# A fused attention and gated-convolution kernel: a new order of TensorE's work, with fp32 runs joined, and a planner rule that marks more row copies as urgent

## The chip, the cores and the metric

One core of one Trainium2 chip runs the whole problem. The metric is the time of one execution on the device in microseconds (us). The kernel before takes 423.37 us, the median of three runs (422.53 to 424.21).

The engines by the names that the profile uses: PE is TensorE (PEld are its weight loads), DVE is VectorE, ACT is ScalarE, POOL is GpSimd, SP is SyncE, which here issues all the transfers but one. "q" behind a name (SPq) is the part of an engine that waits and issues.

## The reference

Agent attention over 4 batches of 12800 positions with 128 channels and 49 agents, followed by a gated convolution over positions:

```python
def _attn_ref(q, k, v, agents):
    a2k = sm(agents, k)                 # softmax over the 12800 keys
    agent_v = a2k @ v                   # 49 x 128
    q2a = sm(q, agents)                 # softmax over the 49 agents
    return q2a @ agent_v

def _moe_ref(x, w_val, conv_w, w_out):  # x is the attention's output
    for k in range(5):                  # causal convolution, 5 taps, per channel
        gate_pre += conv_w[k] * xp[:, k:k + S, :]
    gate = 1.0 / (1.0 + np.exp(-gate_pre))
    val = x @ w_val
    return (gate * val) @ w_out
```

## The kernel before

**Units and chunks.** Each batch is cut into 10 units of 1280 positions for keys, values and queries, and into 25 chunks of 512 positions for the gated convolution. The names in the order string of lines 1103 to 1129 are: `k1.8` the scores of key unit 8 of batch 1, `v` the agents' sums over a value unit, `q` the scores of a query unit and its softmax, `t` the transposition of that softmax, `m` a step of the key maximum, `f` a step that folds a batch's agent values into the convolution's weights, and `g`, `a`, `o` the gate, value and output products of a chunk, numbered 0 to 100 (the last chunk is cut in two).

**What is fp32 and what is 16-bit.** Scores (line 391) and value sums (line 495) multiply fp32 operands; so do the small products of `m` and most of `f`. The gate (lines 937, 941), value (964, 968) and output products (1007 to 1009) and the transposes multiply fp16 operands. A chunk is eleven 16-bit products, each with 512 columns. An fp32 run is a stretch of TensorE's order in which one fp32 product follows another, between two 16-bit ones.

**Banks.** All score units of keys and queries take turns on two PSUM banks (`bank()`, line 252; `sc` in the rows), so a score unit needs the bank of the unit two places ahead of it. A key unit's bank is given back by ScalarE's copy (line 417), a query unit's by VectorE's transpose (line 401). `gate`, `val` and `out` have one bank each: the gate of the next chunk needs the tanh of this one (line 950, ScalarE), its value product needs `h` (line 977, VectorE), and the output product needs `hh` (983, ScalarE) and `hl` (988, GpSimd).

**The path of a query unit.** Scores, transpose on VectorE, maximum, subtraction on GpSimd (765), exponential on ScalarE (773), sums and scaling on VectorE (778 to 787), a 16-bit copy on ScalarE (794) and two rests on GpSimd (800, 808) fill `pt`. From unit 4 of batch 0 on, a transfer transposes `pt` into the rows `x1` (849). Two units are a pair and serve five chunks. Of a pair, two further transfers, the row copies (`shifts`, line 880; issued at 898), set 19 of the rows at five shifts into `x2`, which line 941 multiplies. A pair's copies cover both of its units, but for units 0 to 3 of batch 0, which have copies of their own.

**What sets the order.** TensorE's order is the string. All other steps, the transfers among them, are ordered by `Plan.order` (line 97): it plays the steps through with written-in durations; of the steps that an engine could start now, it takes the one with the largest tail, which is the sum of costs along the longest way from the step to the end. The argument `urge` is added to a step's tail (line 114), and so to the tails of all that lead to it. `SOON` is 10. What comes out is a fixed order per engine, and each engine, and SP's transfer queue, keeps its order: a step that waits holds back all that stand behind it on its engine. At most eight of SP's transfers are on their way at a time; loads go round eleven buffers.

The lines that the change touches:

```python
                src, [("x2", s % 3, o + i * UNIT, r0) for i in range(n)], us * n,
                urge=SOON if g < SINGLE else 0.0,
            )
```

Of the kernel before, what the change touches and what calls it, by code (L numbers as in the profile page):

```python
# [49 lines left out]
SINGLE = 4  # L50
# [13 lines left out]
SOON = 10.0  # L64
# [6 lines left out]
class Plan:  # L71
# [11 lines left out]
    def add(self, engine, us, fn, reads=(), writes=(), moved=0.0, key=None, urge=0.0):  # L83
        i = len(self.steps)
        need = set()
        for x in reads:
            need |= self.wrote.get(x, set())
        for x in writes:
            need |= self.wrote.get(x, set()) | self.read.get(x, set())
        for x in reads:  # L90
            self.read.setdefault(x, set()).add(i)
        for x in writes:
            self.wrote[x], self.read[x] = {i}, set()
        self.steps.append((engine, us, fn, need, moved, key))
        self.urge.append(urge)
# [84 lines left out]
def tile_agent_attention_gated_conv(  # L180
# [10 lines left out]
    B, C, N = qT.shape  # L191
    A = 49
    NU = N // UNIT
# [19 lines left out]
    m2 = const.tile([P, 2], F32, name="m2")  # L213
# [610 lines left out]
    def row_keys(s, halves):  # L824


        i = s % NX
        return [(x, i, h) for h in halves for x in ("x1", "x1b")] + [("x1h", i)] * (0 in halves)

    def halo(s, read=()):  # L830
        to = x1s[s % NX][:, PAD - HALO : PAD]
        if s * 2 % NU == 0:
            fn = lambda: nc.gpsimd.memset(to, 0.0)
        else:
            fn = lambda: nc.gpsimd.tensor_copy(
                out=to, in_=x1s[(s - 1) % NX][:, PAD + SEG - HALO : PAD + SEG]
            )
        keys = [(x, (s - 1) % NX, 1) for x in ("x1", "x1b")]
        add("pool", 0.19, fn, list(read) + keys, [("x1h", s % NX)])

    def transposes(b, u):
# [3 lines left out]
        if not on_pe(b, u):  # L845
            dst = unit_rows(g)
            add(
                "dma", 1.4,
                lambda: nc.sync.dma_start_transpose(
                    out=dst.rearrange("p (n i) -> p n i", i=P),  # L850
                    in_=pt.rearrange("p n r -> p (n r)"),
                ),
                [(*p_, n) for n in range(3)], [("x1", g // 2 % NX, g % 2)], 2.4,
            )
            shifts(b, u)
            return
# [4 lines left out]
        def matmuls():  # L861
# [14 lines left out]
            [at], [("x1b", g // 2 % NX, g % 2)],  # L876
        )
        shifts(b, u)

    def shifts(b, u):  # L880

        g = b * NU + u
        if g >= SINGLE and g % 2 == 0:
            return
        n = 1 if g < SINGLE else 2
        u0 = u + 1 - n
        s = g // 2
        x2, x1 = x2s[s % 3], x1s[s % NX]
        o = (g + 1 - n) % 2 * UNIT
        src = row_keys(s, range(0, g % 2 + 1))  # L890
        c = PAD - HALO + o
        for r0, r1, first, every, us in X2CUTS:
            first += A
            rows = x1[first : first + 1 + (r1 - r0 - 1) * every : every, c : c + 1]
            view = [rows.ap[0], (1, TAPS), (1, n * UNIT)]
            add(
                "dma", 0.6,
                lambda r0=r0, r1=r1, rows=rows, view=view: nc.sync.dma_start(
                    out=x2[X2B + r0 * TAPS : X2B + r1 * TAPS, o : o + n * UNIT],
                    in_=bass.AP(rows.tensor, rows.offset, view),  # L900
                ),
                src, [("x2", s % 3, o + i * UNIT, r0) for i in range(n)], us * n,
                urge=SOON if g < SINGLE else 0.0,
            )
        if g % 2 and g < SINGLE:
            halo(g // 2 + 1)
# [165 lines left out]
    for b in range(B):  # L1072
        t0 = b * NCH
        for i in range(NU):
            g = b * NU + i + LEAD
# [17 lines left out]
    for t in range(len(chunks) + 2):  # L1093
# [9 lines left out]
    order = (  # L1103
# [25 lines left out]
    )  # L1129
    first = [(kinds.get(x[0], x[0]), *map(int, x[1:].split("."))) for x in order.split()]  # L1130
    for w in first:
# [70 lines left out]
```

## Time and profile before

| | |
|---|---|
| median of 3 runs | 423.37 us |
| the profiled execution, its own time | 419.86 us |
| span of its instructions | 417.9 us |
| mean granted TensorE clock | 0.996 |
| PE busy | 399.7 us, 96% |
| ACT busy | 307.2 us, 74% |
| DVE busy | 295.2 us, 71% |
| POOL busy | 237.4 us, 57% |

A row of the timeline gives the start of an instruction (or of a merged group of them, xN) from the span's start, its length, engine, line, operation and tiles; in square brackets stands how long the engine had been idle, and what ended that. Lengths of matmuls overlap, since they are pipelined: how fast TensorE goes is read from one start to the next. A row of waits names who waited, for whom, and how long in total. The page's groups give the busy time and the mean length of one, and then the idle time ahead of them with what ended most of it.

### The profile page before, as it was taken

To read this page: it belongs to the slowest core of one execution; us is meant where nothing else is said; L and a number is where in the kernel's file an instruction comes from. 1 tells how busy PE (TensorE), PEld (TensorE's weight loads), DVE (VectorE), ACT (ScalarE), POOL (GpSimd) and SP (SyncE) were. 2 spreads that over 40 slices of the span, in tenths; PEclk is the share of its full clock that TensorE was granted. 3 is DMA by queue.
4 is the path that set the end of the run, shared out by engine and by line. 5 is a ranking of instruction groups with operands and counts; after the bars stand their busy time and mean duration, and the time that the engine had idled before them with its cause. 6 is when DMAs were issued, how large, how long until landed. Compare 5 with 4: busy or idle time off the path is not lost.

```text
span 417.9 us, 10098 instructions
## 1 busy us (share of the span) xinstructions
PE 399.7 (96%) x3907; PEld 195.2 (47%) x3907; DVE 295.2 (71%) x570; ACT 307.2 (74%) x524; POOL 237.4 (57%) x303
## 2 busy tenths in 40 slices
PE   4978999999999999999999999999999999999995
PEld 1357334336555443345555543344555544344443
DVE  5866889976885977677796685777757598666231
ACT  6584468778957677678987486778877577788775
POOL 1002458655677566564476555585366577787643
PEclk9989999999999999999999999999999999999999
DMA  8999999999999999999999999999999977663823
GB/s 323 418 417 413 356 361 353 303 338 319 413 334 281 284 321 373 354 264 348 352 399 288 279 320 380 295 350 276 323 350 347 271 204 224 187 173 145 247 107 126
DMA packets 75131, 127.63 MB, mean 305 GB/s; under 512 B 50466, under 2 KB 50850, under 8 KB 75084
## 3 DMA queue, kind: packets, MB, share of 16 engines
q1 hardware_dynamic: 74940, 126.87, 96.3%
q8 instruction: 30, 0.49, 0.5%
q10 hardware_dynamic: 144, 0.13, 0.1%
q14 instruction: 17, 0.14, 0.1%
HBM read 79.25 MB, written 26.21 MB: 252 GB/s over the span
## 4 chain that ended last, share of the span: by engine, by line
PE 78%; DMA 11%; DVE 6%; ACT 1%; issue 1%; SPq 1%; POOL 0%; POOLq 0%; DVEq 0%
PE gate L937 24%; PE sc L391 17%; PE av L495 8%; DMA ld<-vP 6%; PE val L964 5%; PE out L1007 5%; PE gate L941 5%; PE val L968 5%; PE out L1008 5%; PE out L1009 4%; DMA ld<-kT 2%; DMA x<-pt 2%; DMA x<-x 1%; DVE h L977 1%; DVE sT L401 1%
## 5 line engine op out<-in xcount | busy, mean ns | idle before, releaser
L988 POOL TENSOR_TENSOR hl<-h,hh 128x512 f16<-128x512 f32 (+1 forms) x101 | 116.7, 1156 | 97.1 <-ACT hh L983 96.8
L937 PE MATMUL gate<-x,stat 128*128 128x512 f16 (+1 forms) x500 | 124.2, 378 | 0.4 <-ACT th L950 0.3
L977 DVE SCALAR_TENSOR_TENSOR h<-th,val 128x512 f32<-128x512 f32 x100 | 67.8, 678 | 62.1 <-PE out L1008 28.3
L391 PE MATMUL sc<-ld,ag_sb 128*32 128x320 f32 x1280 | 101.4, 447 | 7.3 <-DMA ld<-kT 6.7
L950 ACT ACTIVATE th<-gate,unscale 128x512 f32<-128x512 f32 x100 | 68.3, 683 | 32.7 <-PE gate L941 31.3
L1021 ACT ACTIVATE ob<-out,oscale 128x512 f32<-128x512 f32 x98 | 67.2, 686 | 19.1 <-PE out L1009 16.5
L937 PEld LDWEIGHTS <-stat 128*128 128x128 f16 x505 | 46.1, 97 | 63.3 <-issue 13.1
L983 ACT CAST hh<-h 128x512 f16<-128x512 f32 (+1 forms) x101 | 61.4, 608 | 16.6 <-DVE h L977 16.1
L765 POOL TENSOR_TENSOR qw<-sT,qmx 128x490 f32<-128x490 f32 x40 | 41.3, 1034 | 45.0 <-DVE qmx L760 44.7
L391 PEld LDWEIGHTS sc<-ld,ag_sb 128*32 128x32 f32 x1280 | 36.8, 111 | 58.7 <-issue 25.6
L495 PE MATMUL av<-ld,eT 128*32 128x129 f32 (+1 forms) x1400 | 49.6, 276 | 1.5 <-DVE eT L401 1.2
L495 PEld LDWEIGHTS av<-ld,eT 128*32 128x32 f32 (+1 forms) x1400 | 45.6, 115 | 8.4 <-issue 3.0
L808 POOL TENSOR_TENSOR pt<-qw,pt 128x490 f16<-128x490 f32 x40 | 44.8, 1119 | 1.6 <-ACT pt L794 1.4
L401 DVE STREAM_TRANSPOSE sT<-sc 128x640 f32<-128x640 f32 x40 | 33.5, 837 | 12.9 <-PE sc L391 12.2
L486 ACT ACTIVATE e<-ks,kbias 128x320 f32<-128x320 f32 x80 | 39.2, 553 | 3.5 <-DVE eT L401 2.2
L800 POOL TENSOR_SCALAR pt<-qw 128x240 f16<-128x240 f32 x80 | 27.8, 367 | 22.0 <-DVE qw L787 22.0
L401 DVE STREAM_TRANSPOSE eT<-e 128x640 f32<-128x640 f32 x40 | 33.3, 839 | 9.5 <-ACT e L486 5.3
L941 PE MATMUL gate<-x,stat 128*128 128x512 f16 x100 | 37.8, 378 | 0.5 <-DMA x<-x 0.5
L964 PE MATMUL val<-x,stat 128*128 128x512 f16 x100 | 37.9, 379 | 0.2 <-DVE wo L743 0.2
L968 PE MATMUL val<-x,stat 128*128 128x512 f16 x100 | 37.8, 378 | 0.0
L417 ACT COPY ks<-sc 128x640 f32<-128x640 f32 x40 | 27.6, 690 | 13.4 <-PE sc L391 13.0
L1007 PE MATMUL out<-hh,wo 128*128 128x512 f16 x98 | 37.2, 380 | 0.1
(133 smaller groups left out, 418.9 us busy)
## 6 DMA issues: line engine op xcount, KB each, us to landing
ld<-kT SPq DMA_DIRECT2D x40, 640.0 KB
ld<-qT SPq DMA_DIRECT2D x40, 640.0 KB
ld<-vP SPq DMA_DIRECT2D x39, 645.0 KB
outT<-ob SPq DMA_DIRECT2D x48, 512.0 KB
x<-x SPq DMA_DIRECT2D x18, 300.0 KB
x<-x SPq DMA_DIRECT2D x18, 175.0 KB
outT<-ob SPq DMA_DIRECT2D x3, 256.0 KB
ld<-vP SPq DMA_DIRECT2D x2, 322.5 KB
```

What stands on the lines that cost most here:

```text
L391: nc.tensor.matmul(out=out[g * BLK : (g + 1) * BLK, j, 0:GT], lhsT=ag_sb[:, b, j * BLK : (j + 1) * BLK], rhs=src[:, g * GT : (g + 1) * GT] ...
L401: nc.vector.transpose(out=out.rearrange("p n (j i) -> p j n i", j=2), in_=in_.rearrange("p j (n i) -> p j n i", i=BLK),)
L495: nc.tensor.matmul(out=av[o + j : o + j + cols, 0 : C + 1], lhsT=et[:, n, j : j + cols], rhs=vt[:, n, :], start=(u == 0 and n < 2), stop=( ...
L937: nc.tensor.matmul(out=pg, lhsT=stat[:, k, :], rhs=x1[:, c : c + w], start=(k == 0), stop=False,)
L941: nc.tensor.matmul(out=pg, lhsT=stat[:, TAPS + 1, :], rhs=x2[:, o2 : o2 + w], start=False, stop=True,)
L950: lambda: nc.scalar.activation(out=th, in_=pg, func=AF.Tanh, scale=unscale[:, 0:1]),
L964: nc.tensor.matmul(out=pv, lhsT=stat[:, TAPS, :], rhs=x1s[(b * NCH + n0 // CH) // 5 % NX][:, PAD + o2 : PAD + o2 + w], start=True, stop=False,
L968: nc.tensor.matmul(out=pv, lhsT=stat[:, TAPS + 2, :], rhs=x2[:, o2 : o2 + w], start=False, stop=True,)
L977: lambda: nc.vector.scalar_tensor_tensor(out=h, in0=th, scalar=1.0, in1=pv, op0=ALU.add, op1=ALU.mult),
L983: "act", 0.16 + 0.42 * scale, lambda: nc.scalar.copy(out=hh, in_=h),
L988: lambda: nc.gpsimd.tensor_tensor(out=hl, in0=h, in1=hh, op=ALU.subtract),
L1021: lambda: nc.scalar.activation(out=ob[:, o : o + w], in_=po, func=AF.Copy, scale=oscale),
```

## The change

Two things. The order string is written anew: every product is the same, but steps change places, so that fp32 products that stood apart stand side by side. And the row copies that carry `urge` are no longer those of units 0 to 3 alone, but those of units 4 and 5 too, and those of the last pair (units 8 and 9) of batches 0, 1 and 2.

```diff
-                urge=SOON if g < SINGLE else 0.0,
+                urge=SOON if g < SINGLE + 2 or u == NU - 1 and b < B - 1 else 0.0,
...
-        "q0.7 k1.6 o3 k1.7 g5 o4 a5 g6 k1.8 a6 t0.6 t0.7 k1.9 g7 a7 o5 q0.8 m1 g8 a8 o6 m1 g9 "
+        "k1.6 o3 k1.7 g5 o4 a5 g6 a6 t0.6 t0.7 k1.8 k1.9 g7 a7 o5 q0.8 m1 g8 a8 o6 m1 g9 a9 o7 "
```

In the built programs TensorE has 70 fp32 runs before and 56 after; those of them that hold a score or value unit (lines 391, 495) go from 59 to 44, one of the joins having split a small product of `f1` off. Behind the first batch's keys there is one run with more than two score units before (`q0.3 k1.3 k1.4 q0.4`); after there are eight, that one among them. A join moves at most a few steps, over one to four chunks' products.

TensorE, scores of key units 8 and 9 of batch 1, the difference (`sc` the two score banks, `ld` the load buffers, `x_1` rows, `x_` without a further number shifted rows):

```order
 L941 MATMUL gate<-x_106,stat_126 128x512
+L964 LDWEIGHTS stat_126
+L964 MATMUL val<-x_1_102,stat_126 128x512
+L968 LDWEIGHTS stat_126
+L968 MATMUL val<-x_106,stat_126 128x512
 L391 MATMUL sc_135<-ld_64,ag_sb 32x320 x8
-L964 LDWEIGHTS stat_126
-L964 MATMUL val<-x_1_102,stat_126 128x512
-L968 LDWEIGHTS stat_126
-L968 MATMUL val<-x_106,stat_126 128x512
 L391 MATMUL sc_134<-ld_65,ag_sb 32x320 x8
 L937 LDWEIGHTS stat_126
```

The two value products now come ahead of both score units instead of between them.

TensorE, batch 2, key units 0 to 2 and a query unit; before:

```order
L391 MATMUL sc1_135<-ld10_71,ag_sb_145 32x320 x8
L391 MATMUL sc0_134<-ld0_61,ag_sb_145 32x320 x8
L1007 LDWEIGHTS wo160_128
L1007 MATMUL out_138<-hh1_115,wo160_128 128x512
L1008 LDWEIGHTS wo160_128
L1008 MATMUL out_138<-hh1_115,wo160_128 128x512
L1009 LDWEIGHTS wo160_128
L1009 MATMUL out_138<-hl1_118,wo160_128 128x512
L391 MATMUL sc1_135<-ld1_62,ag_sb_145 32x320 x8
L391 MATMUL sc0_134<-ld2_63,ag_sb_145 32x320 x8
```

After:

```order
L1008 LDWEIGHTS wo160_128
L1008 MATMUL out_138<-hh1_115,wo160_128 128x512
L1009 LDWEIGHTS wo160_128
L1009 MATMUL out_138<-hl1_118,wo160_128 128x512
L391 MATMUL sc1_135<-ld10_71,ag_sb_145 32x320 x8
L391 MATMUL sc0_134<-ld0_61,ag_sb_145 32x320 x8
L391 MATMUL sc1_135<-ld1_62,ag_sb_145 32x320 x8
L391 MATMUL sc0_134<-ld2_63,ag_sb_145 32x320 x8
```

The output product (1007 to 1009) stands ahead of all four score units, which follow each other and use the two banks in turn.

ScalarE, chunks 13 to 16, where value units of batch 1 and the query units 8 and 9 of batch 0 meet (`e` exponentials for the values, `qw` those of the queries, `hh`, `th`, `ob` the chunks' own); before, from value unit 1.2 on:

```order
L486 ACTIVATE e0_80<-ks_72,kbias1_76 128x320 x2
L486 ACTIVATE e1_81<-ks_72,kbias1_76 128x320 x2
L486 ACTIVATE e0_80<-ks_72,kbias1_76 128x320 x2
L1021 ACTIVATE ob0_120<-out_138,oscale0_132 128x512
L983 CAST hh1_115<-h1_112 128x512
L950 ACTIVATE th2_110<-gate_136,unscale0_130 128x512
L1021 ACTIVATE ob0_120<-out_138,oscale0_132 128x512
L983 CAST hh2_116<-h2_113 128x512
L486 ACTIVATE e1_81<-ks_72,kbias1_76 128x320 x2
L486 ACTIVATE e0_80<-ks_72,kbias1_76 128x320 x2
L486 ACTIVATE e1_81<-ks_72,kbias1_76 128x320 x2
L773 ACTIVATE qw0_89<-qw0_89 128x490
```

After, from the same unit on:

```order
L486 ACTIVATE e0_80<-ks_72,kbias1_76 128x320 x2
L486 ACTIVATE e1_81<-ks_72,kbias1_76 128x320 x2
L773 ACTIVATE qw0_89<-qw0_89 128x490
L773 ACTIVATE qw1_90<-qw1_90 128x490
L1021 ACTIVATE ob0_120<-out_138,oscale0_132 128x512
L983 CAST hh1_115<-h1_112 128x512
L950 ACTIVATE th2_110<-gate_136,unscale0_130 128x512
L1021 ACTIVATE ob0_120<-out_138,oscale0_132 128x512
```

The exponentials of both query units stand right behind value unit 1.3 now; value unit 1.4 comes after them.

SP, the transfers around the last pair of batch 0 (`x1_0<-pt` the transposes of units 8 and 9, `x21<-x1_0` the pair's row copies); before:

```order
L384 DMA ld10_71<-kT 128x1280
L384 DMA ld0_61<-kT 128x1280
L1036 DMA outT<-ob1_121 128x1024
L384 DMA ld1_62<-kT 128x1280
L849 DMA_TRANSPOSE x1_0_101<-pt0_97 128x10x128
L384 DMA ld2_63<-qT 128x1280
L849 DMA_TRANSPOSE x1_0_101<-pt1_98 128x10x128
L1036 DMA outT<-ob2_122 128x1024
L384 DMA ld3_64<-kT 128x1280
L384 DMA ld4_65<-qT 128x1280
L898 DMA x21_106<-x1_0_101 60x1x2560
L898 DMA x21_106<-x1_0_101 35x1x2560
```

After, from the last load that both have in common:

```order
L384 DMA ld8_69<-vP 128x1290
L849 DMA_TRANSPOSE x1_0_101<-pt0_97 128x10x128
L849 DMA_TRANSPOSE x1_0_101<-pt1_98 128x10x128
L384 DMA ld9_70<-vP 128x1290
L1036 DMA outT<-ob1_121 128x1024
L384 DMA ld10_71<-kT 128x1280
L898 DMA x21_106<-x1_0_101 60x1x2560
L898 DMA x21_106<-x1_0_101 35x1x2560
```

Both transposes and both copies moved up past three loads and two stores of results.

## Rows read from the trace of the kernel before

**Rows 1.** Page, busy time of each engine: us, share of the span, instructions.

```profile
PE 399.7 (96%) x3907; PEld 195.2 (47%) x3907; DVE 295.2 (71%) x570; ACT 307.2 (74%) x524; POOL 237.4 (57%) x303
```

**Rows 2.** Waits of TensorE, whole span: who, us in total, times, longest.

```profile
PE sc L391 <- DMA ld<-kT: 6.7, 4, 5.8
...
PE gate L941 <- DMA x<-x: 0.5, 1, 0.5
...
PE gate L937 <- ACT th L950: 0.3, 2, 0.2
```

**Rows 3.** Timeline, TensorE, a lone score unit: start, length, line, operands.

```profile
158.20 0.38 PE L968 MATMUL val<-x,stat 128*128 128x512 f16 x1
158.51 1.28 PE L391 MATMUL sc<-ld,ag_sb 128*32 128x320 f32 x16
159.72 0.39 PE L1007 MATMUL out<-hh,wo 128*128 128x512 f16 x1
159.95 0.38 PE L1008 MATMUL out<-hh,wo 128*128 128x512 f16 x1
```

**Rows 4.** Timeline, TensorE, two score units in one run.

```profile
171.56 2.36 PE L391 MATMUL sc<-ld,ag_sb 128*32 128x320 f32 x32
173.85 1.25 PE L937 MATMUL gate<-x,stat 128*128 128x512 f16 x5
```

**Rows 5.** Timeline, all engines, first scores: copies of the banks.

```profile
14.38 0.69 ACT L417 COPY ks<-sc 128x640 f32<-128x640 f32 x1 [0.39 <-PE sc L391]
...
15.46 0.69 ACT L417 COPY ks<-sc 128x640 f32<-128x640 f32 x1 [0.38 <-PE sc L391]
...
16.78 1.28 PE L391 MATMUL sc<-ld,ag_sb 128*32 128x320 f32 x16 [0.29 <-DMA ld<-kT]
...
18.12 0.69 ACT L417 COPY ks<-sc 128x640 f32<-128x640 f32 x1 [0.89 <-PE sc L391]
```

**Rows 6.** Page, costliest groups: the two steps that free a score bank.

```profile
L401 DVE STREAM_TRANSPOSE sT<-sc 128x640 f32<-128x640 f32 x40 | 33.5, 837 | 12.9 <-PE sc L391 12.2
...
L417 ACT COPY ks<-sc 128x640 f32<-128x640 f32 x40 | 27.6, 690 | 13.4 <-PE sc L391 13.0
```

**Rows 7.** Timeline, TensorE, four score units in a row, batch 0.

```profile
52.93 2.36 PE L391 MATMUL sc<-ld,ag_sb 128*32 128x320 f32 x32
55.88 2.36 PE L391 MATMUL sc<-ld,ag_sb 128*32 128x320 f32 x32 [0.58 <-DVE sT L401]
```

**Rows 8.** Timeline, TensorE, score units of keys 2.3 and queries 1.5.

```profile
151.89 2.36 PE L391 MATMUL sc<-ld,ag_sb 128*32 128x320 f32 x32
```

**Rows 9.** Timeline, ScalarE, the bank copy that follows.

```profile
153.94 0.69 ACT L417 COPY ks<-sc 128x640 f32<-128x640 f32 x1
```

**Rows 10.** Timeline, weight loads of line 941 that waited.

```profile
93.47 0.10 PEld L941 LDWEIGHTS <-stat 128*128 128x128 f16 x1 [0.37 <-DMA x<-x]
...
134.95 0.10 PEld L941 LDWEIGHTS <-stat 128*128 128x128 f16 x1 [0.18 <-DMA x<-x]
...
233.85 0.10 PEld L941 LDWEIGHTS <-stat 128*128 128x128 f16 x1 [1.00 <-DMA x<-x]
```

**Rows 11.** Chain that ended last: transposes and row copies of units 18, 19.

```profile
219.29 7.52 DMA x<-pt
...
227.84 5.98 DMA x<-x
```

**Rows 12.** Timeline, GpSimd: maximum subtracted from query unit 0.8.

```profile
90.09 1.01 POOL L765 TENSOR_TENSOR qw<-sT,qmx 128x490 f32<-128x490 f32 x1 [1.61 <-DVE qmx L760]
```

**Rows 13.** Timeline, ScalarE: exponentials of values 1.7, then of query unit 0.8.

```profile
104.16 1.01 ACT L486 ACTIVATE e<-ks,kbias 128x320 f32<-128x320 f32 x2 [0.27 <-DVE eT L401]
105.08 0.60 ACT L773 ACTIVATE qw<-qw 128x490 f32<-128x490 f32 x1
```

**Rows 14.** Timeline, TensorE: gates of two chunks in an unbroken 16-bit stretch.

```profile
392.20 1.24 PE L937 MATMUL gate<-x,stat 128*128 128x512 f16 x5
...
394.57 1.24 PE L937 MATMUL gate<-x,stat 128*128 128x512 f16 x5
```

43 rows, old and new, of the table order are left out of this document.

## The prediction

> **What bounds the kernel now.** I read the busy times first. TensorE is busy 399.7 of 417.9 us, 96%, the next engine 74% [rows 1]. The waits of TensorE come second: the largest, 6.7 us in four pieces, is for key loads [rows 2], and one of the pieces stands at 16.78 us [rows 5], in the fill of the pipeline, which the change leaves as it is. What is left is half a microsecond here and there. So TensorE's own sequence sets the end, and a microsecond taken out of it is a microsecond gained, unless a wait opens in its place. Third, the timeline of TensorE, read from start to start: in a long 16-bit stretch a chunk's eleven products take 394.57 - 392.20 = 2.37 us, 0.216 each, and no idle time is noted in front of them [rows 14].
>
> **What an fp32 run costs beyond its work.** A lone score unit lies between 158.20, the last 16-bit product before it, and 159.95, the second one behind it [rows 3]: 1.75 us. Two 16-bit steps in that are 0.43. A further score unit in the same run adds 2.29 - 1.21 = 1.08, from 171.56 to 173.85 against 158.51 to 159.72 [rows 3, 4]. So 1.75 - 0.43 - 1.08 = 0.24 us is the price of going into fp32 and back, paid once a run, however long the run.
>
> The Trainium skill has a sentence that speaks against this: TensorE: Matmul & The Clock Gate, section Step-by-step: what each phase is for, says that the drain of one matmul lies under the fill of the next, so that in a stream only the columns count. By that alone a change of run would cost nothing, and this change would save nothing by it. The 1.75 us of rows 3 say otherwise: 0.24 us are neither columns nor waits.
>
> **The sum.** It is made against the profiled execution's own time, 419.86 us (a span of 417.9 and 1.96 around it); that is 3.51 below the median, 423.37, so what comes out is carried over as a ratio.
>
> 1. *Runs removed.* In TensorE's order the runs with a score or value unit go from 59 to 44: 15 x 0.24 = 3.6 us less. One join leaves a small product of the weight fold standing alone, which the rows do not price in that place; if it costs as much as a run, 14 x 0.24 = 3.4. I take 3.6. That runs with value units pay the same is an assumption.
>
> 2. *The wait for the row copies.* TensorE stood 0.5 us for a row copy [rows 2]. It is the last pair of batch 1: its second transpose takes from 219.29 to 226.81, the copies from 227.84 to 233.82, and the weight load of line 941 goes on at 233.85 [rows 10, 11]. Two more loads of that line waited, 0.37 at 93.47 (units 4 and 5) and 0.18 at 134.95 (last pair of batch 0) [rows 10]. So those pairs have next to no room, and a TensorE that comes 2 us earlier at chunk 45 would wait for nearly all of it. This is what the second half of the change answers. The room is there on ScalarE: query unit 0.8 has its maximum subtracted by 91.10, and its exponential starts at 105.08, behind that of value unit 1.7 [rows 12, 13]. The 14 us between are a choice of the planner. In the new order the exponentials of units 8 and 9 come behind value unit 1.3, four value units earlier, and the transposes and copies move up past three loads and two stores. Four value units are 4 x 1.0 us of ScalarE [rows 13] with the chunk work among them, so I expect the copies some 5 to 10 us earlier, more than the 3.6 us that TensorE gains over the whole run. The 0.5 us go. In exchange the exponentials of value units wait for two of 0.6 us; their matmuls come a chunk or more later, which covers 1.2 us. If the cover failed, it would cost up to 1.2 us in each of three batches.
>
> 3. *The score banks.* This is the new wait. There are two banks, so in a run of three or four score units the third needs the bank of the first 2 x 1.08 = 2.16 us after that one's start. Key units: the copy of the unit that starts at 16.78 starts at 18.12 and takes 0.69, so the bank is free after 2.03 us, and copies at 14.38 and 15.46, 1.08 apart, show that a run of keys keeps its pace when ScalarE is free [rows 5]. When it isn't: unit 2.3, started at 151.89, has its copy at 153.94, 2.05 us later instead of 1.34, so 0.7 late [rows 8, 9]. Query units: VectorE's transpose takes 0.837 instead of 0.690 [rows 6], so the bank is back after 2.18 at best, 0.15 more than a key's. The one such run of before shows the bad end: the third unit of the run from 52.93 was due at 55.09 and started at 55.88 [rows 7]. The seven new long runs hold nine such handovers, seven behind a key unit, two behind a query unit. A key's costs 0 to 0.7, and I take 0.1, near the free ScalarE of rows 5, since the copy has a fixed place in ScalarE's order just there; a query's costs 0.15 to 0.8, and I take 0.3. Together 7 x 0.1 + 2 x 0.3 = 1.3 us (bounds 0.3 and 6.5).
>
> 4. *Chunks without an fp32 run among them.* Where a run leaves, gate, value and output products follow each other and the next gate waits for the tanh of the last. In all, two waits for that cost 0.3 us before [rows 2], and unbroken stretches run without one [rows 14]. I take 0.2 us for new ones (bounds -0.3 and 3). The rest (the maxima, the fold's order on VectorE, loads behind the transposes in SP's queue) lies beside TensorE's 2.37 us a chunk, and I cost it at nothing; if a load were late, TensorE would stand for it one to one.
>
> 419.86 - 3.6 - 0.5 + 1.3 + 0.2 = 417.26, a gain of 2.6 us, 0.62%; of the median, 420.7 us.
>
> **Rivals.** *The banks give it back.* The joined units stand for their banks at 0.4 each instead of 0.14: 9 x 0.4 = 3.6, so 419.86 - 4.1 + 3.6 + 0.2 = 419.56, or 423.1. For it: rows 7 and 9. Against it: nearly all of ScalarE's copies start as soon as the scores end (13.4 us idle over 40 copies, ended by TensorE) [rows 6].
>
> *The copies still hold.* The urgency moves tails in the planner but the transfer lands no earlier, and at chunk 45 TensorE arrives early and waits. Eight of the 15 runs lie ahead of it, so 1.9 us are lost and the 0.5 stays; 7 x 0.24 = 1.7 remain, less 0.6 for four handovers and 0.2: a gain of 0.9, 422.5. For it: rows 10 and 11, three tight places. Against it: the 14 us of rows 12 and 13.
>
> *No price on a run.* If what rows 3 show moved with the units instead of going, step 1 is nothing: 419.86 - 0.5 + 1.3 + 0.2 = 420.86, or 424.4. The sentence of the skill above would say so; the difference of rows 3 and 4 is against it, since the second unit of a run does not pay.
>
> *Slower: ScalarE before the tanh.* A lone fp32 run of 1.2 us between gate and gate is time in which ScalarE, 74% busy, catches up with exponentials, casts and copies. Fifteen such gaps go, and the urgent exponentials now come in pairs. If the tanh comes one 0.6 us step [rows 13] late at two of three of these places, 15 x 0.42 = 6.3 us are lost: 419.86 - 2.6 + 6.3 = 423.56, or 427.1. It turns the change to slower by over 0.5% from a mean of 0.31 us a place. Against it: rows 14, where ScalarE has three steps a chunk and still keeps up, and rows 2.
>
> **How the numbers follow.** The forecast has 68 in 100; its own range is 419.2 (no handover costs more than the least, step 4 at nothing) to 421.8 (the handovers at 2.4). About 0.5%, 2.1 us here, is what a measurement can tell from no change, so faster begins below 421.25, and I give 58 of the 68 to faster, 10 to no change. The banks give it back: 13; the copies still hold: 6; no price on a run: 3; slower by the tanh: 10, of which 1 is within 0.5%. That makes 0.58 faster, 0.33 the same, 0.09 slower. The range leaves out the best tenth and most of the slower case: 418.5 to 424.5.
>
> **What would show it.** Right: in the profile after, TensorE's waits name line 941 and the row copies no more, or by less than 0.2 us; the joined runs show 1.08 us a unit; the exponential of query unit 0.8 starts several microseconds earlier than at 105.08; waits of line 391 for ScalarE's copy or VectorE's transpose come to about 1.3 us. Wrong: line 391 waiting 3 us or more behind the first 60 us (the first rival), line 941 waiting 1 us or more (the second), TensorE's starts behind a run 0.24 us later again although nothing is named (the third), line 937 waiting for the tanh by several microseconds (the fourth). A load named as the releaser behind 60 us would be a cause that I have priced at nothing.

## The result, and the profile after

The changed kernel takes 427.8 us, median of four runs (426.56 to 430.29), against 422.95 for the kernel before: a ratio of 1.015, 95% interval 1.0112 to 1.0188. It is slower by 1.5%, where a gain of 0.6% was forecast, and lies outside the range. Medians, here and below, are of all runs, while ratios leave out runs over 1.5% above the fastest of the same kernel and are not the quotient of two medians (1.0115 here). Repeated later it took 429.27 us against 421.88, a ratio of 1.0158 (1.0108 to 1.0209).

The page of the profile after: busy time of each engine, then two lines of the table in 40 slices (10.6 us each; the granted clock of TensorE and the share of the transfers, in tenths) and the queue of the transfers (packets, MB, share of 16 engines' span).

```profile
PE 402.0 (94%) x3907; PEld 197.9 (46%) x3907; DVE 298.6 (70%) x570; ACT 307.3 (72%) x524; POOL 236.2 (55%) x303
...
PEclk9959999999999999999999899999999999999999
DMA  8999899999999999999999999999999986556723
...
q1 hardware_dynamic: 74940, 126.87, 96.2%
```

The same lines of the kernel before, which the prediction did not use:

```profile
DMA  8999999999999999999999999999999977663823
...
q1 hardware_dynamic: 74940, 126.87, 96.3%
```

TensorE fell from 96% busy [rows 1] to 94% while the span grew by 7.7 us (417.9 to 425.6): it waits. The transfers were as full as TensorE before the change already: 96.3% of 16 engines' span, nine tenths or more in every slice but the first up to about 330 us. The kernel had two bounds, and the prediction read one. The share counts the time that packets took, and they overlap: between 100 and 330 us it is 1.09 before and 1.08 after, so it does not tell what part of a capacity was used; whether the queue is a bound, the experiments with fewer bytes have to show.

TensorE's waits after, the answer to [rows 2]: who, us in total, times, longest.

```profile
PE sc L391 <- DMA ld<-kT: 8.2, 5, 5.9
PE gate L941 <- DMA x<-x: 3.8, 2, 2.7
...
PE sc L391 <- DVE sT L401: 0.9, 2, 0.6
PE gate L937 <- ACT th L950: 0.7, 2, 0.5
...
PE sc L391 <- ACT ks L417: 0.6, 2, 0.3
...
PE val L964 <- DVE h L977: 0.5, 2, 0.3
```

The weight loads of line 941 that waited, from the timeline after, against [rows 10]:

```profile
238.38 0.10 PEld L941 LDWEIGHTS <-stat 128*128 128x128 f16 x1 [3.21 <-DMA x<-x]
...
296.41 0.10 PEld L941 LDWEIGHTS <-stat 128*128 128x128 f16 x1 [1.55 <-DMA x<-x]
...
335.95 0.10 PEld L941 LDWEIGHTS <-stat 128*128 128x128 f16 x1 [0.20 <-DMA x<-x]
```

The waits for row copies that the change was to end are gone at chunks 10 and 20 (93.47 and 134.95 before), and at chunk 45, whose pair (units 1.8 and 1.9) was made urgent, 1.00 us has become 3.21. A pair without urgency (2.4 and 2.5, chunk 60) waits now as well.

What happened to the urgent pair, from the chain after (the answer to [rows 11]): the second transpose, then the last row copy.

```profile
222.00 7.93 DMA x<-pt
230.88 7.46 DMA x<-x
```

The timeline of GpSimd after, the last step that fills `pt` of unit 1.9:

```profile
207.28 1.10 POOL L808 TENSOR_TENSOR pt<-qw,pt 128x490 f16<-128x490 f32 x1
```

The timeline of SP's queue after; a row is the time that issuing takes:

```profile
215.31 10.76 SPq L849 DMA_TRANSPOSE x<-pt  x2
226.16 1.27 SPq L1036 DMA_DIRECT2D outT<-ob  x1
227.52 1.74 SPq L384 DMA_DIRECT2D ld<-kT  x2
229.99 1.68 SPq L898 DMA_DIRECT2D x<-x  x2
```

And, in the kernel before, the step that fills `pt` and SP's issue of the same two transposes:

```profile
211.99 1.09 POOL L808 TENSOR_TENSOR pt<-qw,pt 128x490 f16<-128x490 f32 x1
...
210.64 7.93 SPq L849 DMA_TRANSPOSE x<-pt  x1
...
219.29 2.66 SPq L849 DMA_TRANSPOSE x<-pt  x1
```

The data of unit 1.9 was ready at 208.38, 4.7 us earlier than before (213.08): the urgency worked up to there. But SP began with the pair only at 215.31, 6.9 us after that and 4.7 us later than before (210.64), although the two transposes stand a little earlier in its order now (the 143rd and 144th of 255 transfers, 145th and 147th before). Issuing the two held SP for 10.76 us, about what it did before (7.93 + 2.66 = 10.59). So the second transpose landed at 229.93 instead of 226.81, and the copies at 238.34 instead of 233.82. From ready to landed the second transpose now took 21.6 us instead of 13.7. SP's whole queue ran behind: over its 97th to 142nd transfers it issued 7.0 us later (median) than the kernel before at the same place in the order, 1.8 us of that from the start-up. In the experiments below it was 6.4 us later in the repetition, 0.8 with the order alone, 1.2 with the urgency alone, and with shorter result stores the changed kernel issued 4.5 us earlier than the kernel before. What made it lose the time where it did is not shown. TensorE did not come early either: it stood ready at chunk 45 at 235.17, 2.3 us later than before (232.85).

The wait cost a second time. The windows around it (length, busy times, PEclk, DMA share, GB/s):

```profile
233.00:238.38 5.38, 2.67 (x40) 1.26 (x29) 1.59 (x5) 1.19 (x2) 2.48 (x4) 1.00 1.00 310
238.38:239.51 1.13, 1.12 (x7) 0.83 (x8) 0.00 (x0) 0.64 (x2) 0.00 (x0) 1.00 1.03 424
239.51:242.92 3.41, 3.40 (x10) 1.20 (x9) 2.07 (x7) 1.76 (x4) 1.71 (x2) 0.53 1.02 425
```

TensorE stood for half of the first window. In the third, which begins 1.1 us after it went on, the granted clock was 0.53: nearly all of it at the lower level (1.2 GHz). From the timeline, chunk 46's gate products in that window:

```profile
239.61 2.19 PE L937 MATMUL gate<-x,stat 128*128 128x512 f16 x5
```

They took 2.19 us, against 1.24 at the full clock [rows 14].

**Where the time went.** For each chunk I take the start of its first gate product (line 937) in two traces. The table shows by how many us the difference to the kernel before grew at a place, from the chunk ahead of it; where the new order moves work across chunks, the row is the sum over them. Places where it grew or fell by less than 0.13 in all three are left out, and so are such cells. The profiled execution of before took 419.86 us, 3.1 less than the median, so the 7.7 us between the two spans are more than the 4.9 between the medians. The two other columns are experiments below, in which the transfers have room (thin stores: result stores of a quarter of the length).

| chunk | what lies ahead of it | after | after, thin stores | new order alone, thin stores |
|---|---|---|---|---|
| 0 | start-up: the same instructions in all | +1.83 | +0.99 | +0.49 |
| 5 | units 4 and 5 urgent: score 1.7 waits for a transpose on VectorE | +0.43 | +0.44 | |
| 7 | k1.8, k1.9 joined | -0.24 | -0.23 | -0.23 |
| 10 | a wait for the tanh of before is gone | -0.33 | -0.32 | -0.32 |
| 15 | v1.4, v1.5 joined | +0.38 | +0.38 | +0.29 |
| 22, 23 | four scores joined; last pair of batch 0 urgent | +0.32 | +0.33 | |
| 30 | k2.6, k2.7, q1.7 joined | +0.24 | +0.24 | +0.24 |
| 42 | q2.2, v2.6, v2.7 joined | -0.25 | -0.24 | -0.24 |
| 46 | row copies of 1.8, 1.9 | +2.21 | -0.68 | -0.69 |
| 47 | half clock | +1.69 | | |
| 51, 58 | seven scores joined in two runs | -0.17 | -0.18 | -0.29 |
| 61 | q2.9, v3.0, v3.1 joined; row copies of 2.4, 2.5 | +1.01 | -0.22 | -0.22 |
| 67 | q3.2, v3.5 to v3.7 joined | -0.24 | -0.24 | -0.24 |
| 71 | row copies of 2.8, 2.9 | +0.15 | | |
| 76, 79 | nothing joined | +0.06 | +0.04 | +0.05 |
| 81 | q3.7, q3.8 joined | | | -0.24 |
| 84, 85 | VectorE late for the values | +0.83 | +0.83 | +0.83 |
| 1 to 85 | all, those left out too | +5.83 | -0.02 | -1.25 |

The first two columns differ at chunks 46, 47, 61 and 71 by 2.89 + 1.69 + 1.23 + 0.15 = 6.0 us: that is what the late row copies cost. All other places behind the start-up agree to 0.02 us, but for chunk 11 (0.12).

### The profile page after: what moved, and what is told of

The parts are those of the page before. It is cut to its first block, busy times and chain, and to the rows that moved or that the text cites. A ratio compares the mean times of both kernels' runs of the same rounds, so it can differ in the third digit from the quotient of the medians.

```text
span 425.6 us, 10091 instructions
## 1 busy us (share of the span) xinstructions
PE 402.0 (94%) x3907; PEld 197.9 (46%) x3907; DVE 298.6 (70%) x570; ACT 307.3 (72%) x524; POOL 236.2 (55%) x303
## 4 chain that ended last, share of the span: by engine, by line
PE 58%; DVE 12%; DMA 11%; POOL 9%; issue 5%; ACT 4%; SPq 1%; POOLq 0%; DVEq 0%; ACTq 0%
PE gate L937 16%; PE sc L391 12%; PE av L495 9%; POOL hl L988 5%; DMA ld<-kT 5%; DMA x<-x 4%; PE val L964 3%; PE gate L941 3%; PE val L968 3%; PE out L1007 3%; PE out L1008 3%; PE out L1009 3%; DMA x<-pt 3%; DVE h L977 2%; POOL pt L808 2%
## 5 line engine op out<-in xcount | busy, mean ns | idle before, releaser
L426 DVE TENSOR_REDUCE kmx<-ks 128x2 f32<-128x640 f32 x39 | 31.4, 809 | 9.3 <-ACT ks L417 9.2
```

## The experiments

Times are medians beside the kernel before on the same chip, with the ratio and its 95% interval.

**The two halves apart.** The new order with the old rule:

```diff
-                urge=SOON if g < SINGLE + 2 or u == NU - 1 and b < B - 1 else 0.0,
+                urge=SOON if g < SINGLE else 0.0,
```

> The new order string with the old urgency rule. Theory A (the joined runs move query units 1.6, 1.8, 2.4 and 2.5 to later places, so the transposes and row copies of the pairs 1.8/1.9 and 2.4/2.5 land after their chunk's gate, urgent or not): slower than the kernel before by 0.7 to 1.5%, line 941 waiting 2 us or more for row copies at chunk 45. Rival B (the urgency itself does it: the urgent exponentials and transposes push those of the query units behind them back): the order alone is within 0.6% of the kernel before or faster, and line 941 waits under 1 us.

And the old order with the new rule (the same line, the other way round):

> The old order string with the new urgency rule. Theory A: within 0.4% of the kernel before, the 0.5 us wait at chunk 45 gone or smaller. Rival B: slower by 0.7% or more, with a new wait of line 941 for a pair that has no urgency (the pair 2.4/2.5 or a neighbour). If the two halves add up to less than the 1.5% of both together, it takes both (theory C).

The order alone: 424.54 us, 1.0055 (1.0019 to 1.009), with runs between 421.5 and 429.4. The urgency alone: 421.75, 1.0015 (0.9986 to 1.0044). Neither half gives the 1.5%; by the ratios together they cost more than the sum, though the medians of all runs, 424.54 against 420.95, put the order alone at 0.85%. Where line 941 waited, from the timeline of the order alone:

```profile
96.12 0.10 PEld L941 LDWEIGHTS <-stat 128*128 128x128 f16 x1 [3.44 <-DMA x<-x]
...
332.03 0.10 PEld L941 LDWEIGHTS <-stat 128*128 128x128 f16 x1 [1.53 <-DMA x<-x]
```

and of the urgency alone:

```profile
252.84 0.10 PEld L941 LDWEIGHTS <-stat 128*128 128x128 f16 x1 [0.85 <-DMA x<-x]
...
348.25 0.10 PEld L941 LDWEIGHTS <-stat 128*128 128x128 f16 x1 [0.89 <-DMA x<-x]
```

So it takes both halves for the full loss (theory C). Theory A was right on the urgency, but the order alone cost less than its 0.7%, and it had the place wrong: chunk 45 waits in neither; chunks 10 and 70 do, and chunks 50 and 75. Each variant is late with other pairs.

**Fewer bytes.** The same instructions in the same order, with result stores of a quarter of the length, for the kernel before and for the changed one; three quarters of the result's columns are left unwritten:

```diff
-                out=outT[b, :, n0 + w - n : n0 + w], in_=ob[:, lo : lo + n]
+                out=outT[b, :, n0 + w - n : n0 + w - n + n // 4],
+                in_=ob[:, lo : lo + n // 4],
```

> The kernel before with the result stores cut to a quarter of their columns (the other columns of outT are not written), so that the transfers carry 15% fewer bytes; the planned order is the same. Theory A (the transfers are as near to their limit as TensorE, and row copies land late because of what stands ahead of them): somewhat faster than the kernel before, by 0.5 to 2 us, the wait of line 941 at chunk 45 gone. Rival D (what is lost in the new order are score banks, ScalarE and VectorE): about the same as the kernel before.

> The changed kernel with the same cut of the result stores. Theory A: with room on the transfers the joined runs pay: faster than the cut kernel of before by 1 to 3 us, waits of line 941 below 0.5 us in all. Rival D: still slower than the cut kernel of before by 2 us or more, with waits of lines 391, 937 and 964 for VectorE and ScalarE making it up.

Before, thin: 419.31 us, 0.994 (0.9915 to 0.9965). Changed, thin: 420.13, 0.9963 (0.994 to 0.9986). Fifteen per cent fewer bytes are worth about 0.6% to the kernel before and about 1.9% to the changed one, and its disadvantage shrinks from 1.5% to 0.2%. TensorE no longer waits for the pair 1.8/1.9 or 2.4/2.5. From the page of the changed kernel with thin stores:

```profile
DMA  8999999999999999999998969999997514534501
...
q1 hardware_dynamic: 74940, 107.21, 85.7%
```

and the issue of the two transposes that took 10.76 us above:

```profile
205.35 4.79 SPq L849 DMA_TRANSPOSE x<-pt  x2
```

Number and order of the transfers are the same, so it is not their count but the packets' time that held them up. Theory A's other half fell: with room, the changed kernel is not 1 to 3 us faster than the cut kernel of before, but 0.8 us slower by the medians. Rival D, 2 us or more slower, fell too.

**What the joins are worth with room.** The new order, the old rule (edit as in the first experiment) and thin stores:

> The new order string with the old urgency rule and the result stores cut to a quarter of their columns: what the joined runs are worth where transfers are no limit. From the steps of the profiles (joins 8 x 0.24 us gained, some 1.4 us given back behind ScalarE and VectorE): 0.3 to 0.9 us faster than the kernel before with the same cut. If all fifteen joins pay 0.24 us and nothing is given back: 3.6 us faster. If the joins are worth nothing: the same within 0.2 us.

419.97 us, 0.9937 (0.9909 to 0.9965), not to be told from the 0.994 of before with thin stores. TensorE's starts, the last column of the table, tell more: 1.25 us gained between chunks 0 and 85, against 0.74 for the kernel before with thin stores (0.68 of it the wait at chunk 45). Joins net of what they give back are worth 0.5 us, not 3.6.

**Joins undone.** Three joins behind which starts came later are taken back, with thin stores:

```diff
-a13 g14 a14 o12 t1.0 q1.1 v1.4 v1.5 g15
+a13 v1.4 g14 a14 o12 t1.0 q1.1 v1.5 g15
...
-g28 a28 o26 g29 a29 o27 k2.6 k2.7 t1.6 q1.7 g30
+g28 k2.6 a28 o26 g29 a29 o27 k2.7 t1.6 q1.7 g30
...
-q3.7 q3.8 g80 a80 t3.7 o78 g81
+q3.7 g80 a80 q3.8 t3.7 o78 g81
```

> The new order string with the old urgency, the result stores cut to a quarter of their columns, and three joins undone (v1.4 with v1.5, k2.6 with k2.7, q3.7 with q3.8). Without the scatter of late transfers: if the give-back behind these joins is theirs, 0.5 to 1.1 us faster than the new order with the same cut (in TensorE's starts: 0.29 at chunk 15, 0.24 at chunk 30, 0.6 between chunks 81 and 86). If it is the planner's other steps that moved, TensorE's starts come late at the same places again and the time is the same within 0.3 us.

419.42 us, 0.9957 (0.9939 to 0.9974); times don't tell it from the new order. The starts do, in part: against the new order with thin stores, TensorE is earlier by 0.29 at chunk 15 and 0.24 at chunk 30, exactly what these joins had cost. At the third place 0.63 came back at chunks 84 and 85, but 0.25 went at chunk 81, the price of the run that is there again, and 0.41 was lost at chunks 75 and 76, where the string is the same: there the cost belongs to the other engines' order, which the planner made anew.

**Which urgency.** The new order with urgency for units 4 and 5 alone (`g < SINGLE + 2`), or for the last pairs alone (`g < SINGLE or u == NU - 1 and b < B - 1`):

> The new order string, with the new urgency for units 4 and 5 alone; the last pairs keep none. Theory F (the urgent last pairs push the exponentials of the query units behind them back, 1.0 by five places on ScalarE, 2.0 by six, and with them the transposes in SP's order; that is what costs the changed kernel more than the new order alone): the wait for units 4 and 5 (3.4 us at chunk 10 in the new order alone) goes, chunk 45 waits under 1 us; within 0.3% of the kernel before, or faster. Rival G (the urgency of units 4 and 5 is as bad): 0.8% or more slower.

> The new order string, with the new urgency for the last pairs of batches 0 to 2 alone. Theory F: slow as the changed kernel, 1.0 to 1.8% above the kernel before, line 941 waiting 2.5 us or more for the row copies at chunk 45. Rival G: 0.5% above or less.

426.84 us, 1.0104 (1.0056 to 1.0151), and 425.87, 1.0102 (1.0056 to 1.0149). Theory F fell: both cost the same, and chunk 45 waits in neither. With units 4 and 5 urgent their wait shrank, and the next pair in need waited:

```profile
93.59 0.10 PEld L941 LDWEIGHTS <-stat 128*128 128x128 f16 x1 [0.60 <-DMA x<-x]
...
138.34 0.10 PEld L941 LDWEIGHTS <-stat 128*128 128x128 f16 x1 [3.15 <-DMA x<-x]
...
332.02 0.10 PEld L941 LDWEIGHTS <-stat 128*128 128x128 f16 x1 [1.42 <-DMA x<-x]
```

With the last pairs urgent, units 4 and 5 waited as in the order alone:

```profile
96.17 0.10 PEld L941 LDWEIGHTS <-stat 128*128 128x128 f16 x1 [3.52 <-DMA x<-x]
...
293.12 0.10 PEld L941 LDWEIGHTS <-stat 128*128 128x128 f16 x1 [0.44 <-DMA x<-x]
...
333.25 0.10 PEld L941 LDWEIGHTS <-stat 128*128 128x128 f16 x1 [0.80 <-DMA x<-x]
```

Urgency does not take the wait away, it hands it on: in the five profiles of the new order with full stores and the planner's old prices, line 941's weight loads waited 4.8 to 6.8 us in all for row copies, against 1.55 in the kernel before [rows 10] and 1.74 with the urgency alone.

**The changed kernel again**, for the scatter:

> The changed kernel once more, unchanged, on the chip of the three runs below. Theory A (row copies that come too late when the transfers are full): 1.2 to 1.8% above the kernel before, line 941 waiting 3 us or more in all for row copies, at pairs that need not be the same as in the first profile, since each transfer's landing scatters; the clock of the first 31 us differs from the first profile and has nothing to do with the change. Rival E (the longer low clock at the start comes from the change): low for 10 us near 21 us again.

429.27 us, as above. Its line 941 waited at the same places and a few more:

```profile
238.04 0.10 PEld L941 LDWEIGHTS <-stat 128*128 128x128 f16 x1 [3.80 <-DMA x<-x]
...
336.04 0.10 PEld L941 LDWEIGHTS <-stat 128*128 128x128 f16 x1 [1.77 <-DMA x<-x]
```

The clock fell again right behind the first wait, for 3.41 us. At the start it was low for 6.8 us instead of 10.2, and TensorE was 0.9 late at chunk 0 instead of 1.83. In the fourteen other profiles, where TensorE's instructions up to there are the same, the low stretch was absent or lasted 3.4 or 6.8 us, in the kernel before with prices too; rival E fell.

**A planner that knows the transfers are full.** Its prices are set to the packet times of the trace:

```diff
-                1.57 / len(parts),
+                1.75 / len(parts),
...
-                [(*p_, n) for n in range(3)], [("x1", g // 2 % NX, g % 2)], 2.4,
+                [(*p_, n) for n in range(3)], [("x1", g // 2 % NX, g % 2)], 2.7,
...
-            keys, [], n * 0.00125,
+            keys, [], n * 0.0013,
```

In the changed kernel:

> The changed kernel, the planner's prices of transfers set to what their packets took in the trace (loads 1.57 to 1.75, transposes 2.4 to 2.7, stores 1.28 to 1.33 us): the planner then knows that the transfers are full, and moves the transposes of the pair 1.8/1.9 up by ten places in SP's order. Theory A: line 941 waits less than in the changed kernel at chunk 45 and the time falls by 2 us or more against it. Rival D: the time stays as it is, 427 us.

In the new order with the old rule:

> The new order string with the old urgency rule and the same measured prices of transfers. Theory A: the waits of line 941 fall below 1.5 us in all, and the kernel is at or below the kernel before (within 0.3%). Rival D: as the new order alone, 0.5% slower than the kernel before.

> The new order, the old urgency and the measured prices of transfers once more, on the chip of the other run. If its gain is real: 0.3 to 0.8% faster than the kernel before. If it was the luck of one chip: the same within 0.25%.

In the kernel before:

> The kernel before with the measured prices of transfers alone. If the gain of the new order with these prices (0.6%) is the prices' own: 0.4 to 0.7% faster than before. If it is the joins', set free by the prices: within 0.25% of the kernel before. Estimate: prices 0.3% (the 0.5 us of row copies and some of the run-to-run scatter go), joins 0.3%.

The changed kernel with prices: 425.62 us, 1.0081 (1.0048 to 1.0113). Line 941 no longer waits anywhere, and the time is 2 us below the changed kernel's, as theory A had it, but TensorE has a new wait, for the copy that empties the output bank:

```profile
PE out L1007 <- ACT ob L1021: 3.7, 1, 3.7
```

The timeline of ScalarE at that place:

```profile
322.50 0.61 ACT L773 ACTIVATE qw<-qw 128x490 f32<-128x490 f32 x1 [3.04 <-POOL qw L765]
323.02 0.67 ACT L950 ACTIVATE th<-gate,unscale 128x512 f32<-128x512 f32 x1
323.59 0.68 ACT L1021 ACTIVATE ob<-out,oscale 128x512 f32<-128x512 f32 x1
```

A query unit's exponential stands ahead of the copy in ScalarE's order and waited 3.04 us for GpSimd. The profiled execution took 423.12 us; what the median loses beyond that is not shown.

The new order with prices and without the new urgency: 419.74 us, 0.9939 (0.9913 to 0.9965); again on another chip 419.91, 0.997 (0.9939 to 1.0001). No wait of 0.2 us for row copies in either profile, 416.9 and 416.1 us of span. The kernel before with prices: 419.89, 0.9967 (0.9931 to 1.0003). So the new order with prices is faster than the kernel before by 0.3 to 0.6%, clear of noise in the first measurement and just not in the second; how much of it is the prices' and how much the joins' the intervals don't separate. My estimate of half and half is neither shown nor refuted.

In the old order the prices did not end the waits. The profiled execution of the kernel before with prices was the longest of its twelve (425.36 us), and there line 941 waited 3.1 us for row copies, twice the 1.55 of the kernel before:

```profile
136.93 0.10 PEld L941 LDWEIGHTS <-stat 128*128 128x128 f16 x1 [1.17 <-DMA x<-x]
...
313.96 0.10 PEld L941 LDWEIGHTS <-stat 128*128 128x128 f16 x1 [0.70 <-DMA x<-x]
...
333.43 0.10 PEld L941 LDWEIGHTS <-stat 128*128 128x128 f16 x1 [1.24 <-DMA x<-x]
```

**The same, three joins undone** (the diff of the joins above):

> The new order with the old urgency and the measured prices, three joins undone again (v1.4 with v1.5, k2.6 with k2.7, q3.7 with q3.8), those behind which TensorE's starts came later by 0.29, 0.24 and 0.42 us in the profile. If the give-back belongs to these joins: 0.9 us (0.2%) faster than with them. If it only moves elsewhere: the same within 0.1%.

420.56 us, 0.996 (0.9925 to 0.9995): not told apart from the version with all joins. Two waits for row copies came back at 309.32 (0.16) and 328.35 (0.88).

## Why the prediction was wrong, point by point

*What bounds the kernel* failed first. "A microsecond taken out of it is a microsecond gained" holds where TensorE alone is the limit. The DMA row stood in the same table as the 96%.

*Step 1, a run costs 0.24 us*: right where it can be read by itself. At five places where a run went and nothing followed (chunks 7, 42, 61, 67, 81; the last in the new order alone) the starts moved by 0.22 to 0.25 us, for score runs and value runs alike. For the other ten of the fifteen the price is taken over, not read. The first join, after:

```profile
82.63 0.38 PE L968 MATMUL val<-x,stat 128*128 128x512 f16 x1
82.94 2.36 PE L391 MATMUL sc<-ld,ag_sb 128*32 128x320 f32 x32
85.23 1.04 PE L937 MATMUL gate<-x,stat 128*128 128x512 f16 x4
```

The Trainium skill's sentence (TensorE: Matmul & The Clock Gate, Step-by-step: what each phase is for), that the drain of one matmul lies under the fill of the next, would make a change of run free if it held across fp32 and 16-bit; here it does not hold there, and nor does the third rival.

*Step 3, the score banks, 1.3 us*: right in sum, by luck in its parts. In the new order with thin stores the unit due for a bank started later than 1.10 us behind the one ahead by 0.48 (q1.6), 0.44 (q1.7), 0.14, 0.13, 0.11, 0.05 and three times 0: 1.35 us. But seven handovers behind key units took 1.16 and the two behind query units 0.19; I had 0.7 and 0.6. After, q1.6 in its run:

```profile
162.59 1.26 PE L391 MATMUL sc<-ld,ag_sb 128*32 128x320 f32 x16
164.17 1.28 PE L391 MATMUL sc<-ld,ag_sb 128*32 128x320 f32 x16 [0.32 <-ACT ks L417]
```

*Step 4, 0.2 us*: too small. With thin stores the changed kernel came out at -0.02 us; less 3.6 for the runs, if all fifteen pay, plus 1.2 for the banks (1.35 in the order alone), less 0.68 for the wait at chunk 45, that leaves 3.0 us for all else that moved on ScalarE and VectorE. It is the upper end of my bounds (-0.3 to 3), from which I took nearly the lowest. Of it 1.2 comes with the urgency (the last two columns of the table, -0.02 and -1.25; 0.8 of it at chunks 5, 22 and 23), the rest with the order. Two places after: a gate that follows a chunk without a run, and the value behind the last queries.

```profile
111.22 1.24 PE L937 MATMUL gate<-x,stat 128*128 128x512 f16 x5 [0.46 <-ACT th L950]
...
380.49 0.38 PE L964 MATMUL val<-x,stat 128*128 128x512 f16 x1 [0.32 <-DVE h L977]
```

*Step 2, the row copies, -0.5 us*: the step that failed and turned the sign. Its first half came true, against [rows 12, 13]: unit 0.8's exponential now starts at 98.70, its maximum subtracted by 92.56 (91.55 + 1.01), 6 us of waiting instead of 14.

```profile
98.70 0.60 ACT L773 ACTIVATE qw<-qw 128x490 f32<-128x490 f32 x1
```

But I concluded from an earlier exponential and a higher place in SP's order to an earlier landing, "5 to 10 us". Chunk 20 had that (its copies 2.4 us earlier, start-up included); for the pair 1.8/1.9 the copies landed 4.5 us later. I had counted what each step is moved past, and never when a full queue comes to it: SP began with the pair 4.7 us later, though it stood two places further ahead. With thin stores and the same order it began at 205.35. Late row copies cost 2.21 + 1.69 + 1.23 + 0.15 = 5.3 us (the third is chunk 61 without its join) instead of giving 0.5, and 6.0 against the same kernel with room. The "2 us earlier at chunk 45" of that step did not come either: behind the start-up TensorE was 0.5 us late there, since the joins up to it had been given back.

*The rivals.* "The copies still hold" had the place and the waiting line, and its condition (line 941 waiting 1 us or more) was met. Its time, 422.5, was wrong by 5 us, because it let the copies land when they landed before; it could not become slower. The slower case that I wrote, the tanh, cost 0.7 us by name, not 6.3. The order of magnitude of late copies was in the rows: [rows 10] show three pairs with no room, and every kernel with the new order, the old prices and full stores waited 3 us or more at one of them.

One sum of the numbers is off: the lower end of the own range, 419.2, is what comes out with step 4 at -0.3 or the handovers at nothing; with the handovers at the least and step 4 at nothing, as it is worded, it is 419.5.

What stays open: why SP's queue fell behind where it did, and why a given variant is late at one pair and not at its neighbour. The first 1.83 us of the profiled execution are the start-up clock and no part of the change.

## What to carry to other kernels

Read the DMA row of the profile beside the bottleneck's. Here both stood at 96%, and time saved on TensorE became room to wait for transfers. A scheduler's higher priority for one transfer moved the wait to another pair in each variant of the new order. Setting the planner's prices to measured packet times ended the waits for row copies in the new order, with and without the urgency, but not with three joins undone (1.0 us) and not in the old order (3.1 us), so look at the trace again after it. A joined run gave its 0.24 us at five places; at others a third unit that waited for its bank (0.48 us for q1.6), or ScalarE and VectorE, took it back (behind v1.4 and v1.5 TensorE came 0.29 us later instead of 0.24 earlier).

## What the runs showed of the hardware

- A full queue is not full of bytes. Two windows above moved 424 and 425 GB/s; over the span it is 300 GB/s at 96% busy. The Trainium skill (DMA: Bandwidth & Descriptors, Measured) gives 425 GB/s for a load of 16 MB; the two windows agree. By the packets of the trace of before one of 256 bytes, which the transposes use, took 33 ns on average, one of 5120 bytes 220 ns; 36 transposes of 1280 such packets fill 16 engines for some 96 us, nearly a quarter of the span. The Trainium skill (DMA: Bandwidth & Descriptors, Why small descriptors are slow) says that transfers from on-chip memory to on-chip memory don't pay for small descriptors; these do go from on-chip memory to on-chip memory, and pay three times per byte. Whether that is for the size or for the transposing no run here tells apart.
- Issuing a transpose into a full queue holds SP: 10.76 us for the pair 1.8/1.9 in the changed kernel, 4.79 with thin stores; 7.93 and 2.66 in the kernel before, 1.42 and 1.35 with thin stores. Everything behind it in SP's order waits, loads and stores too.
- A wait of 3.2 to 3.8 us of TensorE's weight loads, with work on both sides, came with 3.4 us at the lower clock level in three profiles (after, its repetition, the last pairs urgent), and with none in two others (3.44 us in the order alone, 3.15 with units 4 and 5 urgent). The wait of 3.7 us for the output bank in the changed kernel with prices came with none either.
